# TensorE's instructions held to the order of the source in a fused attention and MoE kernel

## The chip, the cores and the metric

The kernel runs on one core of a Trainium2 chip. The metric is the device time of one execution in microseconds (µs), the median of several runs. Five engines work side by side, each through its own queue: TensorE (PE, matrix products), VectorE (DVE), ScalarE (ACT), GpSimd (POOL) and SyncE (SP, which issues most of the DMAs). They wait for each other by semaphores.

## What is computed

Three stages follow each other: linear attention with random features, a layer of 512 to 2048 to 512 with a softplus, and a gated layer of 512 to 1024 to 1024 to 512.

```python
def phi(x):                       # q_p, k_p = phi(q_s), phi(k_s)
    h = np.einsum('bhsd,md->bhsm', x, omega) - np.sum(x * x, axis=-1, keepdims=True) / 2.0
    return np.exp(h - np.max(h, axis=-1, keepdims=True)) / np.sqrt(m)
kv = np.einsum('bhsm,bhsd->bhmd', k_p, v)
z = np.sum(k_p, axis=2)
num = np.einsum('bhsm,bhmd->bhsd', q_p, kv)
den = np.einsum('bhsm,bhm->bhs', q_p, z)[..., None] + 1e-06
...
x = np.ascontiguousarray(attn_out.transpose(0, 2, 1, 3)).reshape(B * S, H * D)   # 2304 x 512
h = x @ w_in
x = (np.maximum(h, 0.0) + np.log1p(np.exp(-np.abs(h)))) @ w_out
return ((x @ w1) * (x @ w2)) @ w3 @ w_out2
```

## The kernel before

Every product of 32-bit numbers is made of three: each operand is split into a high and a low half (suffix `h` or `hi`, `l` or `lo`), ACT casts the high one, DVE subtracts to get the low one, and `mm3` (L98) issues hi·hi, hi·lo, lo·hi into one bank of PSUM. PSUM has eight banks, given out by `ps()`.

**Attention.** Tokens come in 18 tiles of 128. `q_feat` projects, `q_turn` transposes (L409), `q_num` multiplies with the sums over keys (`kv`, `qpt`), DVE divides (L426, L427, L430 write `xt`, in two halves, one for each group of four heads), and `x_turn` transposes `xt` in four quarters (L439) into `xs`, which goes to DRAM and is loaded again as `xq`. `fill` puts the first products of the next layer between the last tiles.

**The wide layers.** `widen` multiplies by a two by two scheme of seven products instead of eight (`Quad`). A quad is named (i, c): weight block i, token block c of three. `begin` issues four products of six matmuls (weights `t2`, `t3`, `t1`, `b11`; tokens `s2`, `s3`, `s1`, `a11`), `finish` three more (`t4`·`a22`, `b22`·`s4`, `b21`·`a12`), which go on in the banks of `begin`. In the source `begin` of a quad stands ahead of `finish` of the quad before it. DVE takes the results out of the banks (L517, tiles `u` and `c`), ACT copies the first product (`p`, L524) and makes the softplus (L557).

**Weight blocks.** The halves of a block (`thi`, `tlo` of sums, `hi`, `lo`) come out of a `Job`: a load, two activations (L138, L139), two steps of DVE (L142, L148), sums (L155 to L161), then the casts L187 and L174 on ACT and the differences L191 and L179 on DVE. Jobs stand in a list of closures, and `step(rate)` issues some of them after each product, so that the source mixes them with the products. `until` issues from the list until what a quad needs is there.

**The last layer.** `fold` multiplies w3 with w_out, `w34_ops` splits the result (tiles `th`, `tl`, `bh`, `bl`; casts at L962, differences at L968), and `narrow` multiplies with it. A product there has two banks (e), and each bank takes four blocks of weights (kk), three matmuls for each.

**What sets the order.** The source gives an order of instructions for each engine, and a scheduler that runs when the kernel is built may change it by its own estimate of when operands are ready, with priorities from `tc.high_priority(URGENT)` for the copies out of PSUM. The queues then run in the order that it has set.

Of the kernel before, what the change touches and what calls it, by code (L numbers as in the profile page):

```python
# [71 lines left out]
def body(ctx: ExitStack, tc: tile.TileContext, q, k, k_rest, v, v_rest, om_t, w_in, w_out, w12, w3, wo, out):  # L72
# [227 lines left out]
    def load_k(i):  # L300
        if i < 2 * B:
            raw[i] = K_.tile([128, 2, 512], F32, tag="rawk", bufs=4, name="rawk")
            if i:
                nc.sync.dma_start(out=raw[i], in_=k[i])
            else:
                for t in range(KT):
                    (nc.scalar if t % 2 else nc.sync).dma_start(out=raw[i][:, :, 128 * t:128 * t + 128], in_=k[i][:, :, 128 * t:128 * t + 128])
# [384 lines left out]
        return o, spare_slot  # L692


    nc.scalar.dma_start(out=om, in_=om_t)
    load_k(0)
    nc.scalar.preload_act_table_set("exp_and_others")
# [524 lines left out]
```

## Time and profile before

| | |
|---|---|
| time, median of 3 runs | 812.07 µs (811.88 to 812.77) |
| the profiled execution, its own time | 811.84 µs |
| its span, first to last instruction | 809.7 µs |
| PE busy | 802.7 µs, 99% of the span |
| DVE, ACT busy | 601.1 µs (74%), 440.9 µs (54%) |
| PE's share of the chain that ended last | 93% |

Busy time counts an instruction from its start to its modelled end, and matmuls overlap, so what PE loses is read from the distances between the starts of its matmuls and from its idle times.

### The profile page before, as it was taken

Reading aid. Unit: us, or ns where it says so; the run is one execution under the profiler, and the core shown is the slowest. Engines: PE = TensorE matmul, PEld = TensorE weight load, DVE = VectorE, ACT = ScalarE, POOL = GpSimd, SP = SyncE. Lnnn points to the kernel's source line nnn. Section 1 sums busy time; section 2 is a strip of 40 time slices with the busy share of each in tenths; the row PEclk is TensorE's granted clock in tenths of the full one; section 3 lists DMA queues with packets and bytes.
Section 4 is the critical chain, followed back from the end, with each engine's and each line's share of the span. In section 5 each row is a group of like instructions: output and inputs, shape, how many; then the busy total and the mean of one; then the engine's idle time right before and its main releaser. Section 6 shows DMA issues by size and latency. Waiting matters only on the chain.

```text
span 809.7 us, 14471 instructions
## 1 busy us (share of the span) xinstructions
PE 802.7 (99%) x5462; PEld 751.7 (93%) x5462; DVE 601.1 (74%) x1022; ACT 440.9 (54%) x859; POOL 26.8 (3%) x29
## 2 busy tenths in 40 slices
PE   9999999999999999999999999999999999999998
PEld 8999999999999998888888889999999998889998
DVE  7999999878765675754569633897888876989861
ACT  6999997557545666655456432424335123674330
POOL 3033300000000000000000000000000000000000
PEclk9999999999999999999999999999999999999999
DMA  9833635655535557688994642365646556353212
GB/s 286 318 112 94 196 106 176 230 197 200 208 130 184 195 204 245 219 271 287 327 309 135 223 125 85 124 227 177 216 167 214 189 185 217 126 174 122 71 64 79
DMA packets 75861, 150.04 MB, mean 185 GB/s; under 512 B 7184, under 2 KB 44688, under 8 KB 75792
## 3 DMA queue, kind: packets, MB, share of 16 engines
q1 hardware_dynamic: 64016, 101.55, 37.6%
q10 hardware_dynamic: 11776, 47.57, 17.1%
q8 instruction: 43, 0.70, 0.4%
q14 instruction: 26, 0.21, 0.1%
HBM read 98.24 MB, written 50.86 MB: 184 GB/s over the span
## 4 chain that ended last, share of the span: by engine, by line
PE 93%; DVE 3%; DMA 3%; issue 1%; ACT 0%; ACTq 0%; SPq 0%; DVEq 0%
PE ps L96 90%; DMA xq<-xd 2%; PE ps L409 2%; PE ps L439 1%; DMA rawk<-in_k 1%; DVE s L462 0%; DVE nmax L349 0%; DVE xt L430 0%; DMA xd<-xs 0%; DVE u L517 0%; DVE xs3l L472 0%; DVE c L517 0%; DVE qtl L298 0%; ACT qp L354 0%; DVE s L1027 0%
## 5 line engine op out<-in xcount | busy, mean ns | idle before, releaser
L96 PE MATMUL ps<-dhi,lo 128*128 128x512 f32 x256 | 99.6, 389 | 0.0
L96 PE MATMUL ps<-dlo,hi 128*128 128x512 f32 x256 | 99.6, 389 | 0.0
L96 PE MATMUL ps<-dhi,hi 128*128 128x512 f32 x256 | 99.4, 389 | 0.0
L642 DVE TENSOR_TENSOR dlo<-dn,dhi 128x512 fp32r<-128x512 f32 x64 | 44.0, 690 | 41.8 <-ACT dhi L641 27.5
L517 DVE TENSOR_TENSOR c<-ps,u 128x384 f32<-128x384 f32 x144 | 71.6, 551 | 0.8
L517 DVE TENSOR_TENSOR u<-ps,p 128x384 f32<-128x384 f32 x48 | 26.7, 556 | 54.4 <-PE ps L96 52.8
L641 ACT CAST dhi<-dn 128x512 fp32r<-128x512 f32 x64 | 39.3, 618 | 46.2 <-DVE dlo L642 22.9
L524 ACT COPY p<-ps 128x384 f32<-128x384 f32 x48 | 22.9, 477 | 75.4 <-PE ps L96 56.9
L142 DVE SCALAR_TENSOR_TENSOR f<-raw,f 128x1024 int32<-128x1024 f32 (+2 forms) x43 | 45.2, 1051 | 21.5 <-ACT raw L139 19.9
L557 ACT ACTIVATE c<-c 128x384 f32<-128x384 f32 x72 | 35.0, 525 | 47.9 <-DVE c L517 47.9
L96 PEld LDWEIGHTS ps<-dlo,hi 128*128 128x128 f32 x256 | 48.0, 188 | 10.0
L96 PEld LDWEIGHTS ps<-dhi,hi 128*128 128x128 f32 x256 | 48.0, 188 | 10.0
L96 PEld LDWEIGHTS ps<-dhi,lo 128*128 128x128 f32 x256 | 48.0, 188 | 9.8
L138 ACT ACTIVATE f<-raw,bias 128x1024 f32<-128x1024 int16 (+2 forms) x43 | 46.5, 1089 | 18.0 <-DMA raw<-in_w 9.9
L349 DVE TENSOR_REDUCE nmax<-ps 128x4 f32<-128x512 f32 x72 | 46.7, 682 | 4.3 <-PE ps L96 4.2
L139 ACT ACTIVATE raw<-raw,bias 128x1024 f32<-128x1024 int16 (+2 forms) x43 | 46.4, 1084 | 0.6
L148 DVE SCALAR_TENSOR_TENSOR f<-raw,f 128x1024 int32<-128x1024 int32 (+2 forms) x43 | 45.0, 1047 | 0.6
L354 ACT ACTIVATE qp<-ps,nmax 128x128 f32<-128x128 f32 x144 | 43.0, 478 | 1.9 <-DVE nmax L349 1.9
L354 ACT ACTIVATE kp<-ps,nmax 128x128 f32<-128x128 f32 x128 | 35.7, 492 | 6.0 <-DVE nmax L349 6.0
L96 PE MATMUL ps<-xs1h,thi 128*128 128x384 f32 x96 | 32.3, 337 | 0.3 <-DVE c L517 0.3
L96 PE MATMUL ps<-xs2h,thi 128*128 128x384 f32 x96 | 32.3, 336 | 0.0
L96 PE MATMUL ps<-xs2h,tlo 128*128 128x384 f32 x96 | 32.2, 335 | 0.0
(257 smaller groups left out, 2339.4 us busy)
## 6 DMA issues: line engine op xcount, KB each, us to landing
dn<-gd SPq DMA_DIRECT2D x64, 256.0 KB, 4.2
raw<-in_w ACTq DMA_DIRECT2D x16, 1023.8 KB, 6.0
gd<-c SPq DMA_DIRECT2D x80, 192.0 KB, 2.5
pd<-c SPq DMA_DIRECT2D x48, 192.0 KB, 2.6
raw<-in_w_out ACTq DMA_DIRECT2D x10, 767.8 KB, 4.7
raw<-in_w_in ACTq DMA_DIRECT2D x6, 1023.8 KB, 5.0
rawq<-in_q SPq DMA_DIRECT2D x18, 256.0 KB, 2.9
xd<-xs SPq DMA_DIRECT2D x18, 256.0 KB, 3.3
```

The source lines that it names most:

```text
L96: nc.tensor.matmul(out=o, lhsT=a, rhs=b, start=start, stop=stop, **kw)
L138: nc.scalar.activation(out=self.f, in_=top, func=AF.Relu, scale=TOP, bias=bias[:, 0:1])
L139: nc.scalar.activation(out=self.words(1, F32, 2), in_=top, func=AF.Identity, scale=TOP, bias=bias[:, 1:2])
L142: nc.vector.scalar_tensor_tensor(out=self.f.bitcast(I32), in0=self.words(1, F32, 2), scalar=-2.0 ** 31, in1=self.f, op0=ALU.max, op1=ALU.min)
L148: nc.vector.scalar_tensor_tensor(out=fi, in0=self.words(0, I32, 2), scalar=13, in1=fi, op0=ALU.logical_shift_right, op1=ALU.bitwise_or,)
L349: nc.vector.tensor_reduce(out=nmax, in_=pj, axis=AX.X, op=ALU.max, negate=True)
L354: nc.scalar.activation(out=dst[:, h, :], in_=pj[:, h, :], func=AF.Exp, bias=nmax[:, h:h + 1])
L517: nc.vector.tensor_tensor(out=z, in0=bank, in1=y, op=ALU.add)
L524: nc.scalar.copy(out=p6, in_=b1)
L557: nc.scalar.activation(out=dst, in_=src, func=AF.Softplus)
L641: nc.scalar.copy(out=hi, in_=got[m])
L642: nc.vector.tensor_tensor(out=lo, in0=got.pop(m), in1=hi.bitcast(F32), op=ALU.subtract)
```

## The change

One line is added ahead of the first instruction. It opens a context for the whole program in which the scheduler keeps PE's instructions in the order of the source. The other engines are scheduled as before, but around another order of PE. No operation is added or taken away.

```diff
@@ -692,6 +692,7 @@
         return o, spare_slot
 
 
+    ctx.enter_context(tc.manual_schedule(engines={mybir.EngineType.PE}))
     nc.scalar.dma_start(out=om, in_=om_t)
     load_k(0)
     nc.scalar.preload_act_table_set("exp_and_others")
```

Of PE's 4,835 matmuls 158 stand at another place, in nine pieces. Three of these follow. Numbers of tiles are two higher after the change.

**PE at the first quad with the third weight block, (2, 0).** `thi_2981` and `tlo_2985` are its halves (`thi_2983`, `tlo_2987` after). Before:

```order
L96 MATMUL ps_2937<-xa12l_2731,hi_1514 128x384
L96 MATMUL ps_2937<-xa12h_2730,lo_1569 128x384
L96 MATMUL ps_2993<-xs2h_2178,thi_2981 128x384
L96 MATMUL ps_2993<-xs2l_2179,thi_2981 128x384
L96 MATMUL ps_3006<-xs3h_2017,thi_2981 128x384
L96 MATMUL ps_3006<-xs3l_2018,thi_2981 128x384
L96 MATMUL ps_3015<-xs1h_2175,thi_2981 128x384
L96 MATMUL ps_3015<-xs1l_2176,thi_2981 128x384
L96 MATMUL ps_2993<-xs2h_2178,tlo_2985 128x384
L96 MATMUL ps_2993<-xs2h_2178,thi_2981 128x384
```

With the change, `ps_2872` being the last bank of `finish` of (0, 2):

```order
L96 MATMUL ps_2872<-xa12l_2733,hi_825 128x384
L96 MATMUL ps_2872<-xa12h_2732,lo_839 128x384
L96 MATMUL ps_2995<-xs2h_2180,thi_2983 128x384
L96 MATMUL ps_2995<-xs2l_2181,thi_2983 128x384
L96 MATMUL ps_2995<-xs2h_2180,tlo_2987 128x384
L96 MATMUL ps_2995<-xs2h_2180,thi_2983 128x384
L96 MATMUL ps_2995<-xs2l_2181,thi_2983 128x384
L96 MATMUL ps_2995<-xs2h_2180,tlo_2987 128x384
L96 MATMUL ps_3008<-xs3h_2019,thi_2983 128x384
L96 MATMUL ps_3008<-xs3l_2020,thi_2983 128x384
```

Before, the 18 matmuls of `finish` of (1, 2) (`xa22`, `xs4`, `xa12`) stood ahead of the 24 of `begin` of (2, 0); now they stand behind them. Also, the six matmuls that need `thi` alone no longer stand together.

**PE at the last token tile of the attention.** `xt_2518` (`xt_2520`) is that tile. Before:

```order
L96 MATMUL ps_2532<-xs1h_2175,tlo_796 128x384
L439 MATMUL ps_2547<-ident_78,xt_2518 128x128 x2
L96 MATMUL ps_2559<-xa11h_1908,hi_823 128x384
L96 MATMUL ps_2559<-xa11l_1909,hi_823 128x384
L96 MATMUL ps_2559<-xa11h_1908,lo_837 128x384
L96 MATMUL ps_2559<-xa11h_1908,hi_823 128x384
L96 MATMUL ps_2559<-xa11l_1909,hi_823 128x384
L96 MATMUL ps_2559<-xa11h_1908,lo_837 128x384
L96 MATMUL ps_2579<-xs2h_2178,thi_1352 128x384
L439 MATMUL ps_2547<-ident_78,xt_2518 128x128 x2
L96 MATMUL ps_2579<-xs2l_2179,thi_1352 128x384
```

With the change:

```order
L96 MATMUL ps_2534<-xs1h_2177,tlo_798 128x384
L439 MATMUL ps_2549<-ident_78,xt_2520 128x128 x4
L96 MATMUL ps_2561<-xa11h_1910,hi_825 128x384
L96 MATMUL ps_2561<-xa11l_1911,hi_825 128x384
L96 MATMUL ps_2561<-xa11h_1910,lo_839 128x384
L96 MATMUL ps_2561<-xa11h_1910,hi_825 128x384
L96 MATMUL ps_2561<-xa11l_1911,hi_825 128x384
L96 MATMUL ps_2561<-xa11h_1910,lo_839 128x384
L96 MATMUL ps_2581<-xs2h_2180,thi_1354 128x384
```

The second pair of transpositions moved ahead of seven matmuls.

**PE at the first product of `narrow`.** `ps_8240` and `ps_8241` (`ps_8242`, `ps_8243`) are its two banks, `th_8254` and `tl_8255` (`th_8256`, `tl_8257`) the halves of the fourth block of weights. Before:

```order
L96 MATMUL ps_8240<-xs2h_7909,tl_8183 128x384
L96 MATMUL ps_8241<-xs2h_7895,th_7999 128x384
L96 MATMUL ps_8241<-xs2l_7896,th_7999 128x384
L96 MATMUL ps_8241<-xs2h_7895,tl_8000 128x384
L96 MATMUL ps_8241<-xs2h_7895,th_8095 128x384
L96 MATMUL ps_8241<-xs2l_7896,th_8095 128x384
L96 MATMUL ps_8240<-xs2h_7909,th_8254 128x384
L96 MATMUL ps_8240<-xs2l_7910,th_8254 128x384
L96 MATMUL ps_8241<-xs2h_7895,tl_8096 128x384
L96 MATMUL ps_8241<-xs2h_7909,th_8182 128x384
L96 MATMUL ps_8240<-xs2h_7909,tl_8255 128x384
```

With the change:

```order
L96 MATMUL ps_8242<-xs2h_7911,tl_8185 128x384
L96 MATMUL ps_8242<-xs2h_7911,th_8256 128x384
L96 MATMUL ps_8242<-xs2l_7912,th_8256 128x384
L96 MATMUL ps_8242<-xs2h_7911,tl_8257 128x384
L96 MATMUL ps_8243<-xs2h_7897,th_8001 128x384
L96 MATMUL ps_8243<-xs2l_7898,th_8001 128x384
L96 MATMUL ps_8243<-xs2h_7897,tl_8002 128x384
```

Seven matmuls of the second bank, which stood ahead of and between the three with the fourth block, now stand behind them.

The other pieces: the second pair of transpositions of the token tile before the last moved ahead of five matmuls of `q_num`; the products of (2, 1) and (2, 2) changed places among each other, as did those of two quads of the second wide layer and three matmuls of the layer between. In the second wide layer too, the first quad with the third weight block had three matmuls put in ahead of those that need `tlo`; these now stand later.

On the other engines rows moved as well, but no more than a few places. On SP the second load of the third token block (`xq`, L455) now stands behind two more stores of results (L558). On DVE the sum that waits for this load (`s`, L462) now has the two `u` of its quad ahead of it and the three `c` right behind it; before, a `u` and an `xs3l` (L472) stood between. The difference `xa22l` (L472) of the token block before, which reads the buffer that this load fills, moved behind three `c`. Around the third weight block of the first wide layer neither ACT's nor DVE's rows changed places up to `lo`.

## Rows read from the trace of the kernel before

**Rows 1.** Busy time of each engine, from the page.

```profile
PE 802.7 (99%) x5462; PEld 751.7 (93%) x5462; DVE 601.1 (74%) x1022; ACT 440.9 (54%) x859; POOL 26.8 (3%) x29
```

**Rows 2.** Span and granted TensorE clock of the core.

```profile
core 0: 809.7 us, clock 1.000
```

**Rows 3.** Waits of PE (us in total, times, longest): the longest of seven.

```profile
PE ps L96 <- POOL edge L266: 0.9, 1, 0.9
```

**Rows 4.** Timeline of PE at quad (2, 0): start us, us, instruction.

```profile
168.66 0.33 PE L96 MATMUL ps<-xa22h,thi 128*128 128x384 f32 x1
...
171.82 0.44 PE L96 MATMUL ps<-xs2h,thi 128*128 128x384 f32 x1
172.10 0.34 PE L96 MATMUL ps<-xs2l,thi 128*128 128x384 f32 x1
...
173.08 0.45 PE L96 MATMUL ps<-xs2h,tlo 128*128 128x384 f32 x1
...
176.31 0.33 PE L96 MATMUL ps<-xs2h,thi 128*128 128x384 f32 x1
```

**Rows 5.** Timeline of ACT there.

```profile
170.72 1.04 ACT L187 CAST thi<-t 128x1024 fp32r<-128x1024 f32 x1
```

**Rows 6.** Timeline of DVE there (in brackets idle time and what ended it).

```profile
165.74 0.56 DVE L517 TENSOR_TENSOR u<-ps,p 128x384 f32<-128x384 f32 x1 [0.26 <-PE ps L96]
...
171.80 1.23 DVE L191 TENSOR_TENSOR tlo<-t,thi 128x1024 fp32r<-128x1024 f32 x1 [1.11 <-ACT thi L187]
```

**Rows 7.** Timeline of PE at the last token tile.

```profile
129.44 0.34 PE L96 MATMUL ps<-xs1h,tlo 128*128 128x384 f32 x1
130.14 0.41 PE L439 MATMUL ps<-ident,xt 128*128 128x128 f32 x2 [0.36 <-DVE den L427]
...
131.63 0.38 PE L439 MATMUL ps<-ident,xt 128*128 128x128 f32 x2
131.76 0.42 PE L96 MATMUL ps<-xs2l,thi 128*128 128x384 f32 x1
```

**Rows 8.** Timeline of DVE there.

```profile
128.57 0.16 DVE L426 TENSOR_SCALAR den<-ps 128x4 f32<-128x4 f32 x1 [0.22 <-PE ps L96]
...
130.84 0.42 DVE L430 TENSOR_TENSOR xt<-ps,den 128x256 f32<-128x256 f32 x1
```

**Rows 9.** Timeline of PE at quad (1, 1).

```profile
148.14 0.34 PE L96 MATMUL ps<-xs3h,tlo 128*128 128x384 f32 x1
148.76 0.44 PE L96 MATMUL ps<-xs1h,thi 128*128 128x384 f32 x1 [0.28 <-DVE c L517]
```

**Rows 10.** Timeline of DVE there.

```profile
145.49 0.96 DVE L462 TENSOR_TENSOR s<-xq 128x768 f32<-128x768 f32 x1 [1.54 <-DMA xq<-xd]
...
147.69 1.48 DVE L517 TENSOR_TENSOR c<-ps,u 128x384 f32<-128x384 f32 x3
```

**Rows 11.** Timeline of PE, then of DVE, at the third weight block of the second wide layer.

```profile
540.84 0.33 PE L96 MATMUL ps<-xs3h,thi 128*128 128x384 f32 x1
...
539.65 1.22 DVE L191 TENSOR_TENSOR tlo<-t,thi 128x1024 fp32r<-128x1024 f32 x1
```

**Rows 12.** Timeline of PE, then of DVE, at the first product of `narrow`.

```profile
719.86 0.33 PE L96 MATMUL ps<-xs2h,th 128*128 128x384 f32 x1
...
720.56 0.34 PE L96 MATMUL ps<-xs2l,th 128*128 128x384 f32 x1
721.03 0.45 PE L96 MATMUL ps<-xs2h,th 128*128 128x384 f32 x1
...
722.90 0.33 PE L96 MATMUL ps<-xa11h,bh 128*128 128x384 f32 x1
...
721.13 0.42 DVE L968 TENSOR_TENSOR tl<-wt,th 128x256 fp32r<-128x256 f32 x1
```

**Rows 13.** Timeline of PE at the start, matmuls of one size.

```profile
0.91 2.93 PE L96 MATMUL ps<-edge 128*128 128x256 f32 x6 [0.91 <-POOL edge L266]
...
8.41 1.89 PE L96 MATMUL ps<-om,krest 128*128 128x256 f32 x8
```

## The prediction, made before the changed kernel was run

> **What bounds the kernel now.** I read the busy times first. PE is busy 802.7 of 809.7 µs, DVE 601.1, ACT 440.9 [rows 1, 2]. A busy PE might still be a waiting one, so the waits come next: PE waits seven times in the whole program and the longest takes 0.9 µs, at the very start [rows 3]. Then the distances in the timeline. From 173.08 to 176.31 PE starts 18 matmuls of 128x384 after the first: the first step takes 0.28 (as from 171.82 to 172.10, a first step after a pause), and the other 17 take (176.31 − 173.08 − 0.28) / 17 = 0.174 each [rows 4]. That pace is what the kernel runs at: its time is the number of matmuls times their pace, and PE alone sets it. Nothing in the change alters the count, and a matmul has the same shape wherever it stands, so I expect no change of pace. What can change is waiting. Before, PE hardly waits, so there is little to win (the waits that remain at moved places are 0.3 to 0.4 each), and each µs that PE waits more is a µs of the end, since no pause behind it is long enough to take it up.
>
> So the question is, at each of the nine pieces, whether the operand that now comes first in the queue is there in time. Where the scheduler had put something ahead, I read when the operand landed.
>
> **The change, part by part.**
>
> *Quad (2, 0), the large term.* Before, PE starts `finish` of (1, 2) at 168.66, 18 × 0.174 = 3.1 µs of work, and then meets `thi` of the third weight block at 171.82 [rows 4]. ACT's cast of it runs from 170.72 to 171.76 [rows 5]: the block was only just made, and the 18 matmuls covered its making. With the change PE stands at `thi` at 168.66 with nothing else to do, until 171.82: 3.16 µs. It then has two matmuls (171.82, 172.10), and the third needs `tlo`, which DVE makes from 171.80 to 173.03 [rows 6]; PE starts it at 173.08, as before. Before, four other matmuls with `thi` filled that time. From 173.08 on: one step of 0.28 and 21 of 0.174 over the rest of the 24 of `begin`, so that `finish` of (1, 2) starts at 177.0; its 18 matmuls take 3.13, and the next quad starts at 180.1 instead of 176.31 [rows 4]: **+3.8**. Can `thi` come earlier? Its chain goes back to a result of PE: DVE's `u` at 165.74 waits for PE [rows 6], and behind it DVE makes the sums and the three `c`, on which ACT's softplus waits, ahead of the cast in ACT's queue. That order is unchanged there, so the chain moves with PE and not ahead of it. Bounds: 3.2 (only the wait for `thi`) to 4.2.
>
> *The last token tile.* Before, PE waits for the first half of `xt` until 130.14, runs two transpositions, seven matmuls, the other two transpositions (131.63), and is at the eighth matmul at 131.76 [rows 7]. The second half of `xt` is written from 130.84 to 131.26 [rows 8]; the seven matmuls covered that. With the change all four transpositions come first. DVE's chain may end some 0.25 earlier, because DVE now has work (an `xs3l`) in the 0.22 that it idled at 128.57 [rows 8], so about 131.0. PE sees it about 0.1 later, at 131.1, and the seven matmuls come after: 131.1 + 0.1 for the two transpositions + 0.28 + 6 × 0.174 = 132.5 at the eighth matmul, against 131.76: **+0.8**. Bounds 0.5 to 1.1 (no gain on DVE). The pair of the tile before can wait for at most one such write, 0.42 [rows 8]; it ends beside the work ahead, so I take 0.
>
> *Quad (1, 1).* Before, PE has a step of 148.76 − 148.14 = 0.62, 0.45 over the pace, for a bank that DVE's second `c` frees [rows 9]. The three `c` start at 147.69, held up by the sum that waited for a load until 145.49 [rows 10]. With the change the load is issued later, since the difference that frees its buffer stands behind three `c`: 1.48 by the same three here [rows 10]. But the `c` now follow the sum directly, which takes out one `u` (1.48 / 3 = 0.49) and one `xs3l` (0.96, by the sum of its size): 1.45. The `c` come at about the same time as before, PE comes 0.8 later, so the 0.45 is not waited again: **−0.45**. Bounds −0.45 to +1.0, where the load lands later than that.
>
> *The third block of the second wide layer.* `tlo` ends at 539.65 + 1.22 = 540.87, while PE comes to it at 540.84 [rows 11]. 0.09 of waiting and 0.11 for a first step: **+0.2**. Bounds 0 to 0.9.
>
> *The first product of `narrow`.* PE comes to `th` of the fourth block at 719.86 instead of five matmuls later, and it is there at 721.03 [rows 12]. Then 0.28 to the second, and the third waits for `tl`, 721.13 + 0.42 = 721.55, so 721.6. The 12 of the other bank follow, and the next product starts at 721.6 + 0.2 + 12 × 0.174 = 723.9 instead of 722.90: **+1.0**. Bounds 0.7 to 1.3.
>
> *The other pieces* (products of later quads changing places, three matmuls of the layer between) read operands that are there several µs before they are wanted, and write banks that are freed 25 matmuls, 4.3 µs, behind the matmul that filled them: 0. DVE and ACT, whose rows moved by a few places, have idle time behind which that hides [rows 1]; if that cover were gone at one place, it would cost an eviction, 0.5.
>
> *Sum.* 3.8 + 0.8 − 0.45 + 0.2 + 1.0 = 5.35 µs on the profiled execution's 811.84 (its span is 2.1 shorter). That execution lies 0.23 under the median of the runs, so 812.07 + 5.35 = 817.4, +0.66%.
>
> *A rule weighed against it.* At the start PE's matmuls of 256 columns take 2.93 / 6 = 0.49 each, a little later 1.89 / 8 = 0.24 [rows 13], though the granted clock reads 1.000 over the span [rows 2]. No pause of PE is longer than 0.9 [rows 3], so no row shows what follows one of 3 µs. The Trainium skill, TensorE: Matmul & The Clock Gate, section "Part 1: The HAM clock gate (the 'warmup' mystery)", says that a TensorE that goes idle falls back from 2.4 to 1.2 GHz and needs sustained work to get back; the trace agrees on the slow start and can't test the fall. By the rows the sum is 5.35; by this rule it would be larger, by what the first rival below gives.
>
> **The rivals.**
>
> *The clock falls in the pause at (2, 0).* For it: the pause of 3.2 with 0.8 behind it is far longer than any before. Against it: on both sides of it PE works without a wait over 0.9 [rows 3]. Price: the 22 matmuls behind the second wait at twice their 0.174 would add up to 3.8; I take half, 1.9, as I can't read how long it would last: **819.3**. Beside it stands the rule named above.
>
> *The weight block comes in time* (the other side). If `thi` were made 3.2 µs earlier than before, by a weight job that ACT and DVE take up sooner, the large term would be 0 and the time 812.07 + 1.55 = **813.6**, within 0.2%. It decides from the point where the cast ends by 168.66. Against it: the order of ACT and DVE there and the wait of DVE for PE at 165.74 [rows 6].
>
> *PE does not hold to its queue.* If PE let matmuls with ready operands pass a waiting one, the order would not matter: **812.1**. Against it: at 720.56 PE stands 0.47 − 0.17 = 0.30 for `th` [rows 12], while the third matmul behind the waiting one (`tl_8096`) has an operand of which PE had read the other half already. It did not pass.
>
> *More waits in the crowded places.* The load at (1, 1) lands a µs late, and so on: 818.5, within my range.
>
> **How the numbers follow.** A measurement here can tell 0.2%, 1.6 µs. The forecast, 817.4, has 0.80, the clock 0.08, further waits 0.05 (both slower), the block in time 0.04 (within 0.2%), PE passing 0.02 (the same or a little faster), and 0.01 for a gain that I don't see. Slower 0.93, same 0.05, faster 0.02. The sum of the lower bounds is 3.2 + 0.5 − 0.45 + 0 + 0.7 = 3.95, of the upper 4.2 + 1.1 + 1.0 + 0.9 + 1.3 = 8.5; all at one end is unlikely, and the median itself moves by 0.5. I take 815.4 to 819.6.
>
> **What would show it.** In the profile after, PE should have a new wait of about 3 µs for ACT's `thi` and one of 0.8 for `tlo`, both near 169 to 173; one near 130 to 131 for `xt`; one of about a µs near 720 for `th`; none at quad (1, 1). From there to the end both traces should run at 0.174. I am wrong if the wait for `thi` is missing or much shorter, if PE's pace is slow behind it, or if waits of like size stand at quads that I passed over.

## The result, and the profile after

The changed kernel takes **820.02 µs** (median of 4 runs, 819.59 to 821.83) against 812.15 for the kernel before: ratio 1.0100, 95% interval 1.0083 to 1.0118. That is +7.9 µs where +5.35 was forecast; it lies 0.4 above the top of the range.

Busy time and clock of the profiled execution (819.74 µs) answer to [rows 1, 2]:

```profile
PE 806.0 (99%) x5462; PEld 754.0 (92%) x5462; DVE 603.1 (74%) x1022; ACT 443.5 (54%) x859; POOL 26.5 (3%) x29
core 0: 817.6 us, clock 0.998
```

The trace counts 5,462 matmuls of PE in both kernels (x5462), where the text above has 4,835; nothing rests on that count. PE is "99% busy" in both, so this share hides the loss. The waits of PE (µs in total, times, longest; the longest five) show most of it; before, none was longer than 0.9 [rows 3]:

```profile
PE ps L96 <- ACT thi L187: 3.0, 1, 3.0
PE ps L439 <- DVE xt L430: 1.0, 2, 0.9
PE ps L96 <- ACT th L963: 1.0, 1, 1.0
PE ps L96 <- POOL edge L266: 0.9, 1, 0.9
PE ps L96 <- DVE tlo L191: 0.6, 1, 0.6
```

These are the forecast waits, each at the forecast operand. The timeline of PE at quad (2, 0) answers to [rows 4], that of ACT and DVE (last two rows) to [rows 5, 6]:

```profile
169.81 0.34 PE L96 MATMUL ps<-xa12h,lo 128*128 128x384 f32 x1
173.14 0.45 PE L96 MATMUL ps<-xs2h,thi 128*128 128x384 f32 x1 [2.99 <-ACT thi L187]
173.42 0.34 PE L96 MATMUL ps<-xs2l,thi 128*128 128x384 f32 x1
174.40 0.69 PE L96 MATMUL ps<-xs2h,tlo 128*128 128x384 f32 x1 [0.64 <-DVE tlo L191]
174.88 0.53 PE L96 MATMUL ps<-xs2h,thi 128*128 128x384 f32 x1
175.20 0.53 PE L96 MATMUL ps<-xs2l,thi 128*128 128x384 f32 x1
...
177.12 0.52 PE L96 MATMUL ps<-xs3l,thi 128*128 128x384 f32 x1
177.44 0.38 PE L96 MATMUL ps<-xs3h,tlo 128*128 128x384 f32 x1
177.66 0.34 PE L96 MATMUL ps<-xs1h,thi 128*128 128x384 f32 x1
...
172.05 1.03 ACT L187 CAST thi<-t 128x1024 fp32r<-128x1024 f32 x1
173.12 1.23 DVE L191 TENSOR_TENSOR tlo<-t,thi 128x1024 fp32r<-128x1024 f32 x1 [1.11 <-ACT thi L187]
```

Read the distances: from 174.88 to 177.12 seven steps take 2.24, 0.320 each, where the pace (the distance between the starts of two matmuls) was 0.174; from 177.66 on it is 0.17 to 0.18 again. The rows by stretch (length, busy time of the five engines, then the granted clock, DMA share, GB/s) say why:

```profile
172.00:174.00 2.00, 0.62 (x2) 0.30 (x2) 0.89 (x2) 2.00 (x3) 0.00 (x0) 1.00 0.99 381
174.00:176.00 2.00, 1.60 (x5) 1.60 (x6) 1.16 (x3) 2.00 (x3) 0.00 (x0) 0.52 0.62 225
176.00:178.00 2.00, 2.00 (x9) 2.00 (x8) 1.84 (x3) 0.67 (x2) 0.00 (x0) 0.62 0.00 0
178.00:180.00 2.00, 2.00 (x13) 2.00 (x13) 1.52 (x2) 0.00 (x0) 0.00 (x0) 1.00 0.25 33
```

Behind the pause the granted clock is 0.52, about the lower of the two levels (1.2 instead of 2.4 GHz), and from 178 on it is 1.00 again. PE counts as fully busy while it is slow.

Each trace can be cut at the same eight places of PE's queue (added matmuls not counted). Length of each section in µs (before: cuts at 125.32, 133.06, 154.44, 189.50; then 539.46 to 546.39 and 716.92 to 723.25; all to the last product at 805.76). The kernels below the first rows are the experiments.

| trace | start | last tile | quad (1,1) | quad (2,0) | third block | narrow | the rest |
|---|---|---|---|---|---|---|---|
| before | 125.32 | 7.74 | 21.38 | 35.06 | 6.93 | 6.33 | 603.00 |
| before_again | 126.11 | 7.84 | 20.80 | 35.07 | 6.93 | 6.33 | 602.92 |
| after | 126.38 | 8.59 | 20.80 | 40.29 | 7.27 | 7.39 | 602.92 |
| wide1_only | 126.70 | 7.83 | 20.81 | 41.10 | 6.94 | 6.33 | 602.92 |
| attention_only | 125.19 | 8.60 | 20.80 | 35.07 | 6.93 | 6.33 | 603.27 |
| tail_only | 125.36 | 7.77 | 20.80 | 35.05 | 7.29 | 7.42 | 602.91 |
| filled_pause | 128.36 | 8.50 | 20.80 | 38.85 | 7.28 | 7.41 | 602.95 |
| half_fill | 125.69 | 8.63 | 20.80 | 40.41 | 7.27 | 7.40 | 602.92 |
| finish_first | 127.21 | 8.49 | 20.80 | 35.76 | 7.35 | 7.41 | 603.05 |
| narrow_kk | 126.01 | 8.66 | 20.80 | 40.44 | 7.26 | 5.92 | 603.30 |
| best | 126.98 | 8.16 | 21.10 | 35.74 | 7.27 | 5.91 | 603.45 |
| best_2 | 126.27 | 8.39 | 21.19 | 34.84 | 6.93 | 5.91 | 603.65 |

### The profile page after: what moved, and what is told of

Its sections match the earlier page's. It is cut to its first block, busy times and chain, and to the rows that moved or that the text cites. A ratio compares the mean times of both kernels' runs of the same rounds, so it can differ in the third digit from the quotient of the medians.

```text
span 817.6 us, 14472 instructions
## 1 busy us (share of the span) xinstructions
PE 806.0 (99%) x5462; PEld 754.0 (92%) x5462; DVE 603.1 (74%) x1022; ACT 443.5 (54%) x859; POOL 26.5 (3%) x29
## 4 chain that ended last, share of the span: by engine, by line
PE 88%; DVE 5%; ACT 4%; issue 1%; DMA 1%; SPq 0%; ACTq 0%; DVEq 0%
PE ps L96 86%; ACT kp L354 2%; PE ps L409 2%; DVE nmax L349 1%; DMA rawk<-in_k 1%; PE ps L439 1%; DVE xt L430 1%; DVE kt1h L297 0%; DMA rawq<-in_q 0%; DVE tlo L191 0%; DVE f L148 0%; ACT f L138 0%; ACT raw L139 0%; ACT thi L187 0%; DVE c L517 0%
## 5 line engine op out<-in xcount | busy, mean ns | idle before, releaser
L187 ACT CAST thi<-t 128x1024 fp32r<-128x1024 f32 x16 | 17.1, 1069 | 28.8 <-PE ps L96 25.8
```

## The experiments

**The pieces one by one.** Source order for TensorE around one call, `widen(Up1, ...)`:

```diff
-    widen(Up1, win, ("X0", "X0", "X1"), after_1, lambda: next(d1), begun)
+    with tc.manual_schedule(engines={mybir.EngineType.PE}):
+        widen(Up1, win, ("X0", "X0", "X1"), after_1, lambda: next(d1), begun)
```

> Source order for TensorE inside the first wide layer alone; everything else as the scheduler of the kernel before has it. Theory (pause and clock): the pause at quad (2,0), 3.0 us on thi and 0.64 us on tlo, and some ten matmuls at 0.32 instead of 0.174 us behind it make +5.2, so about 817.3, with a stretch of granted clock near 0.5 behind the pause. Rival (pause alone, the rest of the measured 7.9 us came from the start): +3.8, about 815.9, granted clock 1.00 throughout. Second rival (pieces are not additive): under +3.

817.79 (4 runs; 812.09 before), ratio 1.0059, 1.0038 to 1.0080. The section of quad (2,0) grows by 41.10 − 35.07 = 6.0, more than in the changed kernel. Here the low clock begins at the first matmul behind the wait and lasts longer:

```profile
169.38 0.34 PE L96 MATMUL ps<-xa12h,lo 128*128 128x384 f32 x1
172.71 0.69 PE L96 MATMUL ps<-xs2h,thi 128*128 128x384 f32 x1 [2.98 <-ACT thi L187]
173.19 0.52 PE L96 MATMUL ps<-xs2l,thi 128*128 128x384 f32 x1
173.97 0.69 PE L96 MATMUL ps<-xs2h,tlo 128*128 128x384 f32 x1 [0.25 <-DVE tlo L191]
...
178.29 0.52 PE L96 MATMUL ps<-xs1h,thi 128*128 128x384 f32 x1
```

So the wait for `thi` alone was enough here, and the price differs between the two traces. It seems to differ between runs of one kernel too: the changed kernel's slowest run (821.83) has a mean clock of 0.996, its other three 0.998; here the profiled run has 0.996, the other three 0.998.

The same line ahead of the first instruction, but closed again when `widen` comes to quad (2, 0):

```diff
+            if m == 6 and begun:
+                pe_order.close()
```

> Source order for TensorE from the start up to quad (1,2), the two token tiles included; quad (2,0) and all behind it as the scheduler likes. Theory (sum of the terms as placed, the start's 1.06 us being chance): +0.9 at the last token tile, -0.6 at quad (1,1), together +0.3, about 812.4. Rival (the change itself makes the start 1.06 us longer, by the other engines' order): +1.4, about 813.5, and the first product of attention weights by values starts near 14.8 instead of 13.6 us.

813.65 (10 runs; 812.09), ratio 1.0015, 1.0004 to 1.0027. The last tile costs 8.60 − 7.84 = 0.8, as forecast; the start, in the same order as in the changed kernel, is this time shorter than before's. The median, +1.56, is nearer to the rival's 813.5 than to the theory's 812.4. The trace can't say where the 0.8 beside the tile lies, since the profiled run (812.28) is the fastest of the ten; the longer start, which the rival asks for, is not in it, and the second trace of before (below) has one with the old order.

And the line ahead of `widen(Up2, ...)`, from there to the end:

> Source order for TensorE from the second wide layer to the end alone. Theory (terms add): +0.3 at the third weight block of the second wide layer and +1.0 at the first product of the narrow layer, +1.3, about 813.4. Rival (these waits lie beside other slack): within 0.3 us of the kernel before.

813.49 (10 runs; 812.09), ratio 1.0017, 1.0008 to 1.0027: third block +0.36, narrow +1.09. The terms add: 0.59 + 0.15 + 0.17 = 0.91% against 1.00% for the whole change, within its interval.

**Work in the pause.** Ahead of the first product of quad (2, 0):

```diff
+            for _ in range(fill):
+                matmul(bank, xh[:, 0, 0:128], xh[:, 0, :], True, True)
```

> The changed kernel with 16 matmuls more, on operands that are there already, ahead of quad (2,0)'s first product, whose first matmul overwrites their sums: 16 x 0.174 = 2.8 us of work in a pause of 3.0 us, which takes nothing away from the wait itself. Theory (the pause lets TensorE's clock fall and that costs 1.5 us): the kernel with more work is the faster one, about 818.5 against 820.0, and the granted clock stays at 1.00 behind the pause. Rival (the slow matmuls behind the pause come from memory that the weight splits use at the same time, not from the clock): unchanged, 820.0, the ten matmuls still at 0.32 us.

> The changed kernel with 8 matmuls more in the pause, of no use to the result, instead of 16: 1.4 us of work and then an idle stretch of some 1.6 us on thi and 0.6 us on tlo. Theory A (the fall comes with the length of the idle stretch, and one half as long is not enough): clock 1.00 behind the pause, as with 16, about 818.6. Theory B (any stretch above a microsecond lets it fall): granted clock near 0.5 and matmuls at 0.32 us behind the pause, about 820.0.

With 16: 818.65 (4 runs; 812.09), 1.4 below the changed kernel although it has more to do. The ranges overlap: its highest run, 820.24, is the profiled one, in which the clock fell elsewhere (last section). The other three have a mean clock of 1.000, where the changed kernel's four have 0.996 to 0.998. The section decides:

```profile
171.88 2.94 PE L96 MATMUL ps<-xs2h 128*128 128x384 f32 x16
175.04 0.44 PE L96 MATMUL ps<-xs2h,thi 128*128 128x384 f32 x1 [0.22 <-ACT thi L187]
175.31 0.34 PE L96 MATMUL ps<-xs2l,thi 128*128 128x384 f32 x1
176.30 0.44 PE L96 MATMUL ps<-xs2h,tlo 128*128 128x384 f32 x1 [0.64 <-DVE tlo L191]
176.57 0.34 PE L96 MATMUL ps<-xs2h,thi 128*128 128x384 f32 x1
```

`thi` comes no sooner and the wait for `tlo` is still there, but the pace behind is 0.17, and the section grows by 38.85 − 35.06 = **3.79**: the forecast's 3.8 without the clock. The rest of the changed kernel's 40.29, 1.44, is the clock. The rival (memory that the weight splits use at the same time) is out: ACT and DVE make the same splits here, and PE is not slow.

With 8: 819.46 (4 runs; 812.19). PE idles 1.60 and 0.65, and the clock fell all the same in the profiled run (section 40.41); theory A is refuted there:

```profile
172.00:174.00 2.00, 0.86 (x3) 0.56 (x4) 1.23 (x1) 2.00 (x3) 0.00 (x0) 1.00 0.93 352
174.00:176.00 2.00, 2.00 (x8) 2.00 (x8) 1.31 (x3) 2.00 (x3) 0.00 (x0) 0.56 0.29 109
176.00:178.00 2.00, 2.00 (x8) 2.00 (x8) 1.97 (x2) 0.04 (x1) 0.00 (x0) 0.58 0.05 18
```

The four runs have mean clocks of 0.997, 0.997, 0.999 and 1.000, so with the half fill it does not seem to fall in each.

**The written order mended, TensorE still in source order.** One call moved in `widen`:

```diff
+                    if m == 6 and begun:
+                        quads.pop(m - 1).finish()
                     quads[m].begin()
```

> The changed kernel with two calls swapped in the source at one place: the end of quad (1,2), 18 matmuls, stands ahead of the beginning of quad (2,0), so source order now fills the pause with work that was there anyway. Theory (the written order is what costs, not TensorE in a fixed order as such): 18 x 0.174 = 3.1 us cover the wait of 3.0 us for thi and nearly all of that for tlo, the granted clock stays at 1.00, and of the 5.2 us nothing above 0.3 is left, about 814.9. Rival (other engines' work is held back by the swap and comes due later): a new wait of over 1 us at one of the next quads, about 816 or more.

815.50 (4 runs; 812.19); clock 1.000 in all four. Of the 5.22 at quad (2, 0) 0.70 is left, not 0.3: PE comes to `thi` without a wait (173.88), but still stands 0.64 for `tlo`, as in the changed kernel: DVE makes `tlo` out of `thi` from 173.86 to 175.09, and only two matmuls on `thi` stand ahead of the first on `tlo`. The new wait of over 1 µs, the rival's sign, is not there.

In `narrow`, for the first product:

```diff
-            for e in range(2):
-                for kk in range(2 * NG):
+            turns = [(e, kk) for e in range(2) for kk in range(2 * NG)]
+            if c == 0 and ww == "t2":
+                turns.sort(key=lambda x: x[1])
+            for e, kk in turns:
```

> The changed kernel with the loops of the narrow layer's first product turned round in the source: over the four weight pieces outside and over the two output halves inside, so that 18 matmuls instead of 9 stand ahead of the last weight piece. Theory (TensorE stands 1.0 us at this piece because half of the ready work is written behind it): the wait goes and the tail is 1.0 us shorter, about 819.0. Rival (the piece only moves with it, since its chain starts from what TensorE finishes): the wait stays at 1.0 us, 820.0.

818.99 (4 runs; 812.19). The section falls from 7.39 to 5.92, 0.4 below before; 0.38 of it is given back in "the rest". The net 1.1 is the forecast's.

Both, and the first quad's last six matmuls ahead of the last tile's transpositions:

> The changed kernel with all three places mended in the source: the end of quad (1,2) ahead of quad (2,0), the narrow layer's first product with the weight pieces outside, and the last part of the first quad's beginning, six matmuls, ahead of the last token tile's transposes. Theory (the whole loss is the written order at these places): -5.2, -1.0 and -0.8 from 820.0 give 813.0, and against the kernel before, whose own waits there were 0 to 0.4 us, within 0.2% of it. Rival (a fixed order as such costs something that these places do not show): 814.5 or more.

814.49 (11 runs; 812.19), ratio 1.0027, 1.0016 to 1.0037: the rival's figure, not the theory's 813.0. The trace shows places for most of it. At quad (2, 0) 0.67 is left, the wait for `tlo`; at the third block 0.34, which was not touched; at quad (1, 1) there is 0.3 more, the wait of [rows 9] come back. The tile is mended by half only: DVE's first addition on the bank of these six matmuls now came ahead of `xt`.

```diff
+        if t == nt + XLAG - 1:
+            next(begun[1])
```

is the tile's part of the last version (only the six matmuls come first, their additions later); in quad (2, 0) the twelve matmuls on `thi` of its first three products stand ahead of the six on `tlo`, and `finish` comes first at the third block of the second wide layer too.

> The kernel with all three places mended, and mended better: ahead of the last token tile's transposes now stand the six matmuls alone, without the three additions on VectorE that got in front of xt there; in quad (2,0) the twelve matmuls on thi stand ahead of the six on tlo; and the end of the quad before stands ahead of the third weight block's first quad in the second wide layer too. Theory (what is left of the loss are three written places): -0.7, -0.6 and -0.3 from 814.5 give 812.9, within 0.2% of the kernel before at 812.2. Rival (a fixed order costs what no single place shows): unchanged, 814.5.

813.05 (12 runs; 811.87), ratio 1.0014, 1.0002 to 1.0025. Quad (2,0) and the third block are back at before's lengths or below; the tile is not:

```profile
131.60 0.38 PE L439 MATMUL ps<-ident,xt 128*128 128x128 f32 x2
132.99 0.44 PE L439 MATMUL ps<-ident,xt 128*128 128x128 f32 x2 [1.00 <-DVE xt L430]
...
131.18 0.96 DVE L462 TENSOR_TENSOR s<-xq 128x768 f32<-128x768 f32 x1 [0.37 <-DMA xq<-xd]
132.05 0.55 DVE L517 TENSOR_TENSOR u<-ps,p 128x384 f32<-128x384 f32 x1
132.52 0.41 DVE L430 TENSOR_TENSOR xt<-ps,den 128x256 f32<-128x256 f32 x1
```

DVE, which the scheduler still orders, has a sum and an addition ahead of `xt`. The sum stood there before too, but now waited 0.37 for its load; the addition is new and belongs to the six matmuls, so the wait moved with the work meant to cover it. The tile's 0.55 is not all: quad (1, 1) is 0.39 longer than in the second trace of before, and "the rest" 0.73, of which 0.37 follows the turned product of `narrow`, which itself gains 0.42, and 0.3 stands at 573, in the second wide layer. At quad (1, 1) the sum waited for a load again, and PE has a step of 0.45 (rows of PE, then of DVE):

```profile
149.74 0.34 PE L96 MATMUL ps<-xs3h,tlo 128*128 128x384 f32 x1
150.19 0.44 PE L96 MATMUL ps<-xs1h,thi 128*128 128x384 f32 x1
...
148.25 0.96 DVE L462 TENSOR_TENSOR s<-xq 128x768 f32<-128x768 f32 x1 [1.52 <-DMA xq<-xd]
```

No version beats the kernel before.

**The kernel before once more.**

> The kernel before once more, for a second trace. Theory (the start and the short wait at quad (1,1) differ from run to run by themselves): the wait of 0.5 us at quad (1,1) of the first trace is missing or of another size, as in the run with only the tail in source order, and the time at the first matmuls of the token tiles lies up to 1 us off the first trace's. Rival (both belong to the order of the kernel before): the same wait, and the same times to 0.2 us.

812.10, one run. Its start is 0.79 later than in the first trace, and the section of quad (1,1) is 20.80 instead of 21.38, as in tail_only, which has the old order there too, and in most kernels with the new one. Both differences belong to the run.

## Why the prediction missed

- *The large term, +3.8*: right. The measured one is 3.79 where the clock is held up, and the waits (2.99, 0.64) are the forecast ones.
- *The step that failed: "The clock falls in the pause at (2, 0)", chance 0.08, left out of the sum.* It fell in every profiled run with a pause of 3 µs (after, wide1_only, narrow_kk; the mean clock of all twelve runs of these kernels is 0.996 to 0.998, and never under 0.999 in the kernel before) and cost 40.29 − 38.85 = 1.44 in the changed kernel and 41.10 − 38.85 = 2.25 in wide1_only, against the rival's price of 1.9. What I set against it, that PE works without long waits on both sides, says nothing about a pause of 3 µs: no row of before had one. That no row could show the effect was a reason to widen the range, not to give it 0.08. The prediction's own sign of being wrong, a slow pace of PE behind the wait for `thi`, is what came. The rule cited there (the Trainium skill, TensorE: Matmul & The Clock Gate, "Part 1: The HAM clock gate (the 'warmup' mystery)"), that an idle TensorE falls back to the lower clock, stands: these traces agree, with 0.52 behind the pause.
- *Quad (1, 1), −0.45*: not an effect of the change, as far as the traces show. Against the first trace of before the section does shrink, by 0.58, but the second trace and tail_only have 20.80 with the old order, and best and best_2 have the wait back with the new one (steps of 0.35 and 0.45 instead of 0.174, behind sums that waited 1.35 and 1.52 for their load). It goes with when the load lands and when PE comes, and both differ from run to run; the term was read from one trace. What sets the landing is open.
- *Last token tile, +0.8*: 8.59 − 7.84 = 0.75 (attention_only 0.76). *Narrow, +1.0*: 1.06. *Third block, +0.2*: 0.34. *The other pieces, 0*: "the rest" is 602.92 in both.
- *The sum.* 0.75 + 5.22 + 0.34 + 1.06 = 7.37 against the second trace of before; the start's 0.27 makes up the 7.64 between the two traces. Forecast 5.35 + 1.44 (clock) + 0.45 (quad (1,1)) = 7.24 is within 0.13 of the sum. The medians' 7.9 is the same within the runs' spread; which part of the remaining 0.3 is the start can't be told, as that varies by more (125.19 to 127.21 where the order is one and the same).
- The rivals "PE does not hold to its queue" and "the weight block comes in time" are out by the waits of 1.0 for `th` and 2.99 for `thi`.

## What to carry to other kernels

A scheduler's order on the bottleneck engine can hide what the source order does not: before fixing the order, list where an operand that comes first in the source is made last, and write independent work ahead of it. A pause of PE can cost more than its length: behind the one of 3 µs here came a slow stretch of 1.4 to 2.3 µs more. If such a pause can't be filled with useful matmuls, useless ones can get that second part back (1.44 of the section here). And a wait that is to be "saved" should be seen in two traces before it is put into a sum.

## What was unexpected of the hardware

The clock's fall varies in place and length: in the changed kernel it shows after the second wait, in wide1_only at the first matmul. It does not need 3 µs: in half_fill it came after 1.60 and 0.65, and in filled_pause's profiled run elsewhere, after a wait of 1.27 with little work around it, in the token tiles:

```profile
102.00:104.00 2.00, 0.98 (x6) 0.78 (x6) 2.00 (x9) 1.77 (x4) 0.00 (x0) 1.00 0.03 10
104.00:106.00 2.00, 1.89 (x10) 1.92 (x11) 2.00 (x9) 1.97 (x8) 0.00 (x0) 0.62 0.46 131
106.00:108.00 2.00, 2.00 (x12) 2.00 (x11) 2.00 (x3) 1.75 (x5) 0.00 (x0) 0.53 0.00 0
```

That run's start (128.36) carries it. The wait of 1.00 at `narrow`, with full work on both sides, left the clock at 1.00.
